# Fetching gathered rows two jobs ahead and running the last batch's transform beside the first expert jobs

## Chip, cores and metric

The kernel runs on one core of a Trainium2 chip. The metric is the device time of one execution in microseconds (us); lower is better.

## What is computed

For `x` of shape (8, 1856, 256) the reference takes the real part of a two-dimensional Fourier transform of each batch, and sends every one of the 14,848 result rows through a two-level mixture of experts:

```python
X = np.fft.fft(np.fft.fft(x, axis=1), axis=2).real     # 8 x 1856 x 256 -> 14848 rows of 256
g = argmax(X @ w_group); e = argmax(X @ w_expert[g])   # 4 groups x 4 experts
h = np.maximum(X @ w1[g, e], 0.0)                      # 256 -> 1024
out[row] = softmax_g * softmax_e * (h @ w2[g, e])      # 1024 -> 256
```

## The kernel before

**Phase 1** (`phase1`) goes through eight batches of 1856 rows. Per batch: `fold` uses the transform's symmetries on VectorE, `s_stage` multiplies by cosine and sine tables (`pu`), `d_stage` does the second transform and the router's logits (`pr`, `pl`), `rows` copies the results into row tiles on ScalarE, and `route` picks expert and place of each row with a chain of small VectorE operations and one group of matmuls (`misc<-oh`), and writes every row to its expert's part of a DRAM table `XS` with indirect DMAs from GpSimd (`scatter`, 14 or 15 tiles of 128 rows a batch). The order of the pieces is written out by hand in strings (`START`, `ORDER0`, `ORDER`, `ORDER7`, `ORDER8`); one letter is one step of one generator. `d_stage` and `route` of batch b run during the `s_stage` of batch b+1; those of the last batch run in a ninth turn with nothing beside them but the first expert's preparation.

**Phase 2** (`phase2`) is a list of *jobs*, each of up to four slots; a slot is 128 rows of one expert. Experts 0 and 1 have early jobs on rows of the first batches (`waves`); every expert has seven fixed slots, from expert 2 on as a job of four and a job of three; twelve overflow slots have weights of their own and come one before each of the experts 2 to 13. A job needs its rows gathered from `XS` into tiles `xg` (a pool of `XGB` buffers), split into two fp16 halves `xh` (a cast on ScalarE, a subtraction on VectorE), and transposed by DMA into `xT` (`turn_steps`); then `layer1` (48 matmuls, `ph`, whose ReLU result `hT` ScalarE and VectorE split) and `layer2` (24 matmuls a slot, `py`, then `y` on ScalarE and an indirect DMA `out<-y`). In the loop of `phase2`, job n runs `layer1(n)` and then `layer2(n-1)`, and meanwhile `prep(n+1)`. `slot_weights` reads each row's weight and number out of `xg` at the start of its job, so an `xg` buffer is held until then. Weights (2 MB an expert, `wst<-w`) are loaded by SyncE, squared and summed on ScalarE (`junk`), and split into fp16 halves (`whl`: a cast on ScalarE, a residual on VectorE).

The helper `InOrder` keeps the order of phase 1 as written; most of phase 2 is ordered by the framework's scheduler ahead of time. On the chip each engine's queue, POOL's and SP's too, is worked through in that order.

```python
g = prep(n + 1)
xT, xgs, ges = xs.pop(n)
cw, toks = self.slot_weights(qp, xgs, ges, inv)   # last reader of job n's xg tiles
next(g, None)                                     # issues the gathers of job n + 1
hT = finish(self.layer1(hp, w, xT, len(slots)), lambda: tick(g, T1 * len(slots)))
```

Of the kernel before, what the change touches and what calls it, by code (L numbers as in the profile page):

```python
# [19 lines left out]
NE, F = 16, 1024  # L20
# [13 lines left out]
XGB = 10  # L34
# [14 lines left out]
START = 'GHGGGZdGHHHGU'  # L49
ORDER0 = 'SSiFSYUYiisFFFFGYSIsilsFFIsFYUdlZRFSSIiRZF'  # L50
ORDER = 'ssRdZFdZsDIDSLStSFlIZZFFDlNDlLZdRlRLRdsNRRSURIRXSdIdRFDiNRLSdDsUdXZSsldtIsNsR'
ORDER7 = 'ISSiZsdDdLZFZDLLZNDZDDDdlDdNWRLIRSWRRsRUDRSRSdIdRSsXSRRiiWlXIRUsRsWRSRsiSRWRXWR'
ORDER8 = 'XIDDiLWXDRWlRLIDDDXDdWRLRRdRdRLtdRURDRRRRRXDDRRRRRRRSRdZXXWXWRW'
# [202 lines left out]
class K:  # L256
# [314 lines left out]
    def nyquist_rows(self, b, U, up):  # L571
# [5 lines left out]
        for i in range(2):  # L577
            self.A.activation(un[:, i], self.UN[:, i], AF.Copy, scale=rat[0:B, 0:1])
            if i:
                if b % 2 == 0:  # L580
                    self.Um[b // 2] = up.tile([P, 2, 2, P], F16, name="Um")
# [83 lines left out]
    def route(self, b, pl):  # L665
# [19 lines left out]
        dd = sm.tile([P, nt, 2, 4], F32, name="dd")  # L685
        mx = sm.tile([P, nt], F32, name="mx")
        m4 = sm.tile([P, nt, 4], F32, name="m4")
# [17 lines left out]
        pe = sm.tile([P, nt, 4, 4], F32, name="pe")  # L705
# [3 lines left out]
        es = sm.tile([P, nt, 4], F32, name="es")  # L709
# [16 lines left out]
        oh = sm.tile([P, 4, 4, nt], F16, name="oh")  # L726
# [19 lines left out]
        op = sm.tile([P, NE, nt], F32, name="offp")  # L746
# [41 lines left out]
    def phase1(self):  # L788
        tc, nc, cp, ps = self.tc, self.nc, self.cp, self.ps
        with tc.tile_pool(name="xq", bufs=4) as xp, tc.tile_pool(name="fft", bufs=1) as fp, \  # L790
                tc.tile_pool(name="u", bufs=2) as up, tc.tile_pool(name="row", bufs=1) as rp:
# [28 lines left out]
            n = waves()[-1][2]  # L820
            for e in range(NEARLY):
                nc.sync.dma_start(
                    out=self.XS[e * CAP:e * CAP + n * P].rearrange("(s p) c -> p s c", p=P),
                    in_=bc(xg[:, :].bitcast(I32), 1, n))

            def run(gens, order, rest=True, keep="N"):

                for k in order:
                    if k == "R":
                        for j in "ZLD":  # L830
                            for _ in gens.pop(j, None) or ():
                                pass
                    if k in self.queues:
                        if self.queues[k]:
                            self.queues[k].pop(0)()
                    elif gens.get(k):
                        next(gens[k], None)
# [11 lines left out]
            for b in range(B + 1):  # L849
# [5 lines left out]
                g["N"] = F  # L855
                if b == W0_AT:
# [5 lines left out]
                if b < B:  # L862
                    Us[b] = up.tile([P, 2, 2, NK], F16, name="U")
                    g["S"] = self.s_stage(b, Us[b])
                    g["U"] = self.nyquist_rows(b, Us[b], up)
# [4 lines left out]
                else:  # L870
                    pl = ps.tile([P, NT * 40 + 20], F32, name="pl", tag="lg")
                    self.row_tiles(b - 1, xp)
                    g["D"] = self.d_stage(b - 1, Us[b - 1], pl)
                    g["L"] = self.leftovers(b - 1, Us.pop(b - 1))
                    g["R"] = self.route(b - 1, pl)
# [4 lines left out]
                order = {0: ORDER0, B - 1: ORDER7, B: ORDER8}.get(b, ORDER)  # L880
                run(g, order, keep="NWXR" if Z else "NWX" if b < B else "N")
            run({}, "sIidddd")


# [163 lines left out]
    def turn_steps(self, qp, xgs, V, A, Q, most=4, bufs=(3, 4)):  # L1048

        n = len(xgs)  # L1050
        xT = qp.tile([P, 4, most * P], F16, name="xT", bufs=bufs[0])
        xT = xT[:, :, 0:n * P]
        for j, xg in enumerate(xgs):
# [3 lines left out]
            V.tensor_tensor(out=xh[:, 1], in0=xg[:, 0:D], in1=xh[:, 0], op=ALU.subtract)  # L1057
# [3 lines left out]
        return xT  # L1061

    def turn(self, qp, xgs):
        return finish(self.turn_steps(qp, xgs, self.nc.vector, self.nc.scalar, self.nc.sync))

    def first_turn(self):
# [4 lines left out]
        self.xT0 = yield from self.turn_steps(self.xp0, self.xg0, self.V, self.A, self.Q, w[2] - w[1], (1, w[2] - w[1]))  # L1071
# [41 lines left out]
    def slot_weights(self, qp, xgs, ges, inv):  # L1113

        t = qp.tile([P, 4], F32, name="cws", bufs=4)
        k = qp.tile([P, 4], I32, name="tok", bufs=4)
        for j, (xg, ge) in enumerate(zip(xgs, ges)):
            self.V.tensor_scalar(out=t[:, j:j + 1], in0=xg[:, D + 1:D + 2], scalar1=inv[:, 0:1], scalar2=None,
                                 op0=ALU.mult)
            self.V.scalar_tensor_tensor(out=k[:, j:j + 1], in0=ge, scalar=BIG, in1=xg[:, D:D + 1],  # L1120
                                        op0=ALU.mult, op1=ALU.add)
        return [[a[:, j:j + 1] for j in range(len(xgs))] for a in (t, k)]

    def phase2(self, wp):
        tc, nc = self.tc, self.nc
        wpa = self.wpa
        with tc.tile_pool(name="wo", bufs=1) as op, \
# [163 lines left out]
```

## Time and profile before

| | us |
|---|---|
| median of 3 runs | 950.77 (947.7 to 952.43) |
| the profiled execution, its own time | 956.92 |
| its span | 955.1 |
| PE busy | 837.9 (88%) |
| ACT, DVE, POOL busy | 597.8, 540.3, 409.7 |

PE is TensorE, ACT ScalarE, DVE VectorE, POOL GpSimd, SP SyncE (which only issues DMAs here). Busy time is a sum over the span; which wait holds PE up in which stretch is read from the waits and the timeline. The granted clock is a share of TensorE's full 2.4 GHz; 0.50 is its lower level, 1.2 GHz.

### The profile page before, as it was taken

What the parts mean: (1) busy time and instruction counts of PE and PEld (TensorE: products, weight loads), DVE (VectorE), ACT (ScalarE), POOL (GpSimd) and SP (SyncE); (2) the same over time, 40 slices, a digit from 0 to 9 for tenths busy, and PEclk for the clock granted to TensorE, in tenths of its full rate; (3) what the DMA queues carried; (4) which work ended last, traced back from release to release, by engine and by line L of the source; (5) the groups of instructions that cost most, each with busy time, mean ns of one, the idle gap of its engine ahead of it and who ended that gap; (6) DMA issues with size and microseconds to landing.
All of it is one profiled execution on the core that took longest, in us unless ns stands there. A gap on an engine that the chain in (4) does not pass through costs nothing. (4 is left out here: it accounts for less than half of the span.)

```text
span 955.1 us, 18094 instructions
## 1 busy us (share of the span) xinstructions
PE 837.9 (88%) x6567; PEld 592.5 (62%) x6567; DVE 540.3 (57%) x1342; ACT 597.8 (63%) x1238; POOL 409.7 (43%) x374
## 2 busy tenths in 40 slices
PE   3798889939798899998898989998999998999996
PEld 1465556717486485757575757575757575766765
DVE  6398775653535766464646555555555655574530
ACT  3477677843657877665767676666666667674631
POOL 1018788777045253434343434343534352533212
PEclk9799999969799999999999999999999999999999
DMA  9824554476725675747474646565656564534001
GB/s 353 282 101 169 194 195 133 149 185 231 255 65 143 196 225 90 225 81 212 81 217 88 205 93 192 109 188 119 185 122 192 116 216 89 163 76 91 34 17 38
DMA packets 110171, 145.95 MB, mean 153 GB/s; under 512 B 76368, under 2 KB 81773, under 8 KB 108288
## 3 DMA queue, kind: packets, MB, share of 16 engines
q1 hardware_dynamic: 92752, 99.96, 36.3%
q0 software_dynamic: 16896, 44.60, 17.3%
q8 instruction: 52, 0.85, 0.4%
q14 instruction: 39, 0.32, 0.1%
q10 hardware_dynamic: 432, 0.22, 0.1%
HBM read 97.18 MB, written 33.29 MB: 137 GB/s over the span
## 5 line engine op out<-in xcount | busy, mean ns | idle before, releaser
L1083 PE MATMUL ph<-xT,whl 128*128 128x384 f16 (+3 forms) x2304 | 378.9, 310 | 40.9 <-DVE hT L1087 26.6
L1099 PE MATMUL py<-whl,hT 128*128 128x256 f16 x2976 | 377.1, 274 | 8.1 <-ACT hT L1086 4.3
L1099 PEld LDWEIGHTS <-hT 128*128 128x128 f16 x2976 | 287.3, 98 | 76.5 <-issue 11.4
L1083 PEld LDWEIGHTS <-whl 128*128 128x128 f16 x2304 | 198.9, 99 | 167.4 <-issue 45.3
L779 POOL DMA_INDIRECT out<-y,tok x124 | 134.5, 1084 | 335.4 <-ACT y L1104 236.0
L1087 DVE SCALAR_TENSOR_TENSOR hT<-ph,hT 128x128 f16<-128x128 f32 (+3 forms) x384 | 184.2, 498 | 117.8 <-ACT hT L1086 114.2
L1086 ACT ACTIVATE hT<-ph 128x128 f16<-128x128 f32 (+3 forms) x384 | 162.3, 446 | 62.9 <-PE ph L1083 60.4
L1042 POOL DMA_INDIRECT xg<-XS,ii_s x100 | 115.0, 1150 | 101.9 <-DVE tok L234 73.6
L234 DVE SCALAR_TENSOR_TENSOR whl<-wst,e_v,whl 128x1024 f16<-128x1024 f32 x112 | 138.8, 1278 | 16.8 <-ACT whl L234 16.0
L1055 ACT CAST xh<-xg 128x256 f16<-128x256 f32 x121 | 48.4, 402 | 154.4 <-DMA xg<-XS,ii_s 89.7
L1057 DVE TENSOR_TENSOR xh<-xg,xh 128x256 f16<-128x256 f32 x121 | 50.7, 422 | 153.5 <-ACT xh L1055 153.5
L234 ACT ACTIVATE whl<-wst,e_v 128x1024 f16<-128x1024 f32 x112 | 122.3, 1139 | 5.7 <-DVE e_v L234 5.6
L234 ACT ACTIVATE junk<-wst 128x1024 bf16<-128x1024 f32 x112 | 118.6, 1059 | 7.7 <-DMA out<-y,tok 6.6
L1104 ACT ACTIVATE y<-py,cws 128x256 f32<-128x256 f32 x124 | 58.1, 474 | 55.5 <-PE py L1099 31.9
L234 PE MATMUL pu<-CS,ghl 128*128 128x464 f16 (+3 forms) x384 | 86.2, 377 | 3.4 <-ACT ghl L234 3.4
L779 POOL DMA_INDIRECT XS<-whl,posi x42 | 50.8, 1210 | 75.1 <-ACT row L234 62.7
L234 PEld LDWEIGHTS <-ghl 128*128 128x128 f16 (+1 forms) x384 | 45.5, 122 | 35.6 <-issue 6.4
L234 PE MATMUL pr<-c,U 128*128 128x256 f16 x336 | 47.7, 278 | 11.7 <-ACT whl L234 6.8
L779 POOL DMA_INDIRECT XS<-row,posi x45 | 51.2, 1137 | 13.6 <-issue 13.1
L234 PEld LDWEIGHTS <-U 128*128 128x128 f16 x672 | 43.3, 98 | 21.2 <-issue 12.9
L234 DVE TENSOR_TENSOR xq<-xq 128x1028 f32<-128x1028 f32 x32 | 38.9, 1224 | 6.7 <-DMA xq<-xq 6.6
L234 ACT CAST U<-pu 128x464 f16<-128x464 f32 (+3 forms) x64 | 32.0, 539 | 6.3 <-PE pu L234 6.1
(148 smaller groups left out, 449.8 us busy)
## 6 DMA issues: line engine op xcount, KB each, us to landing
wst<-w SPq DMA_DIRECT2D x108, 512.0 KB
xq<-xq SPq DMA_DIRECT2D x14, 1028.0 KB
CS<-cs SPq DMA_DIRECT2D x8, 464.5 KB
xq<-xq SPq DMA_DIRECT2D x4, 514.0 KB
wst<-w SPq DMA_DIRECT2D x8, 256.0 KB
xT<-xh SPq DMA_TRANSPOSE x124
out<-y,tok POOLq DMA_INDIRECT x124, 2.8
xg<-XS,ii_s POOLq DMA_INDIRECT x100, 2.9
```

Source lines behind the costliest of these rows:

```text
L234: return self.tc.keep_in_program_order(f(*args, **kw))
L779: ins = self.nc.gpsimd.indirect_dma_start(out=out, out_offset=bass.IndirectOffsetOnAxis(ap=ap, axis=0), in_=in_, in_offset=None, bounds_ch ...
L1042: self.nc.gpsimd.indirect_dma_start(out=xg[:, :].bitcast(I32), out_offset=None, in_=self.XS[:, :], in_offset=bass.IndirectOffsetOnAxis(ap= ...
L1055: A.copy(xh[:, 0], xg[:, 0:D])
L1057: V.tensor_tensor(out=xh[:, 1], in0=xg[:, 0:D], in1=xh[:, 0], op=ALU.subtract)
L1083: nc.tensor.matmul(ph[:, 0:n * P], lhsT=w[:, wl, o:o + P], rhs=xT[:, xl * 2 + c, :], start=i == 0, stop=i == 5)
L1086: nc.scalar.activation(hT[:, f, 0], ph[:, 0:n * P], AF.Relu)
L1087: nc.vector.scalar_tensor_tensor(out=hT[:, f, 1], in0=ph[:, 0:n * P], scalar=0.0, in1=hT[:, f, 0], op0=ALU.max, op1=ALU.subtract)
L1099: nc.tensor.matmul(py, lhsT=hT[:, f, hl, j * P:(j + 1) * P], rhs=w[:, wl, 2048 + f * D:2048 + (f + 1) * D], start=i == 0, stop=i == 23)
L1104: nc.scalar.activation(y, py, AF.Copy, scale=cw)
```

## The change

1. **Rows.** `turn_steps` now also writes a small tile `wt` (each row's number and weight) right after the split, and `slot_weights` reads that; an `xg` buffer is free once its row tile is split. The gathers are moved out of `prep` into `fetch`, which is called for job n+2 at the start of job n. `XGB` falls from 10 to 8. VectorE's small operations go from two a slot to one a slot and two a job.
2. **Memory.** Pools stand on two stacks. The row tiles of the last batch lie on the right, and the right stack is given to `wo` (overflow weights) and `w2s` (raw weights of odd experts from 3) once they are written out; the tiles of the expert jobs take the left space of the transform's tables. The raw weights of expert 1 use the buffer of expert 0.
3. **The last batch.** The ninth turn is gone. `last_rows` steps through `ORDER8` (a `|` ends a step), one step at each `tick` of the first expert jobs. The early jobs now alternate between experts 0 and 1 from the first.
4. **Order.** New order strings; the two DMAs that fill `XS` come a little later; some small pools have one buffer in place of two.

```diff
-XGB = 10
+XGB = 8
-START = 'GHGGGZdGHHHGU'
+START = 'HGGdHGGHHZGUG'
...
-ORDER8 = 'XIDDiLWXDRWlRLIDDDXDdWRLRRdRdRLtdRURDRRRRRXDDRRRRRRRSRdZXXWXWRW'
+ORDER8 = 'sIi|LDD|dDLi|D|sLd|DDL|D|Dd|R|dRR|d|R||R|R|D||RRRR|D|R|RDRdR||R|R|R|RR||||RRLR'
...
             V.tensor_tensor(out=xh[:, 1], in0=xg[:, 0:D], in1=xh[:, 0], op=ALU.subtract)
+            tw = V.scalar_tensor_tensor(out=wt[:, j], in0=ges[j].broadcast_to([P, 2]), scalar=BIG,
+                                        in1=xg[:, D:D + 2], op0=ALU.mult, op1=ALU.add)
...
-    def slot_weights(self, qp, xgs, ges, inv):
+    def slot_weights(self, qp, wt, inv):
+        n = wt.shape[1]
...
+        self.V.tensor_scalar(out=t[:, 0:n], in0=wt[:, :, 1], scalar1=inv[:, 0:1], scalar2=None, op0=ALU.mult)
+        self.V.tensor_copy(out=k[:, 0:n], in_=wt[:, :, 0])
...
+    def last_rows(self):
+        yield from self.run(self.last, ORDER8)
+        for _ in self.last["R"]:
+            pass
+        self.late.close()
...
-            for e in range(NEARLY):
-                for _, r0, r1 in w[:2]:
-                    jobs.append((e, "e", [(e, r) for r in range(r0, r1)]))
-            for _, r0, r1 in w[2:]:
+            for _, r0, r1 in w:
                 for e in range(NEARLY):
...
+                    return "wo", "wo"
+                return ("w2s" if e % 2 and e > 1 else "w"), ("w2" if e % 2 else "wa")
...
             def tick(g, t):
...
                 next(g, None)
+                tail()
...
+            fetch(0)
             finish(prep(0))
+            fetch(1)
...
                 g = prep(n + 1)
-                xT, xgs, ges = xs.pop(n)
-                cw, toks = self.slot_weights(qp, xgs, ges, inv)
-                next(g, None)
+                xT, wt = xs.pop(n)
+                cw, toks = self.slot_weights(qp, wt, inv)
+                fetch(n + 2)
```

Three places show how the instructions move. A number behind a name tells one tile from the next.

**First place: POOL and ACT between two experts in mid-run.** POOL before: scatters of a three-slot job's outputs (`y_5324`, `y_5354`, `y_5384`) and the gathers (`xg`).

```order
L779 DMA out<-y_5324,tok_4931 14848x256
L779 DMA out<-y_5354,tok_4931 14848x256
L1042 DMA xg_5816<-XS_80,ii_s_3537 128x260
L1042 DMA xg_5820<-XS_80,ii_s_3537 128x260
L1042 DMA xg_5824<-XS_80,ii_s_3537 128x260
L1042 DMA xg_6018<-XS_80,ii_s_3537 128x260
L1042 DMA xg_6022<-XS_80,ii_s_3537 128x260
L779 DMA out<-y_5384,tok_4931 14848x256
L779 DMA out<-y_5542,tok_5190 14848x256
```

ACT before, in the four-slot job that follows: the casts `xh` of those gathers stand between the ReLUs `hT`, one output behind the gathers.

```order
L1086 ACTIVATE hT_5411<-ph_5412 128x512
L234 ACTIVATE junk_5423,wacc_5422<-wst_4369 128x1024
L1055 CAST xh_5861<-xg_5816 128x256
L1086 ACTIVATE hT_5411<-ph_5428 128x512
L234 ACTIVATE junk_5423,wacc_5422<-wst_4369 128x1024
L1055 CAST xh_5883<-xg_5820 128x256
L1086 ACTIVATE hT_5411<-ph_5440 128x512
L1055 CAST xh_5905<-xg_5824 128x256
```

POOL now, at the like place (`y_4764` and `y_4794` are outputs of a three-slot job, `y_5089` to `y_5194` those of the next four-slot job).

```order
L781 DMA out<-y_4764,tok_4330 14848x256
L1059 DMA xg_5573<-XS_80,ii_s_3393 128x260
L1059 DMA xg_5577<-XS_80,ii_s_3393 128x260
L1059 DMA xg_5581<-XS_80,ii_s_3393 128x260
L781 DMA out<-y_4794,tok_4330 14848x256
L1059 DMA xg_5585<-XS_80,ii_s_3393 128x260
L781 DMA out<-y_4942,tok_4599 14848x256
L1059 DMA xg_5842<-XS_80,ii_s_3393 128x260
L1059 DMA xg_5846<-XS_80,ii_s_3393 128x260
L781 DMA out<-y_5089,tok_4800 14848x256
```

ACT now, where the casts of these gathers stand.

```order
L1127 ACTIVATE y_5160<-py_5135,cws_4799 128x256
L1127 ACTIVATE y_5194<-py_5169,cws_4799 128x256
L236 ACTIVATE whl_5165<-wst_4593,e_v0_5129 128x1024 x4
L1073 CAST xh_5866<-xg_5573 128x256
L1073 CAST xh_5889<-xg_5577 128x256
L1073 CAST xh_5912<-xg_5581 128x256
L1127 ACTIVATE y_5354<-py_5329,cws_4949 128x256
L1109 ACTIVATE hT_5234<-ph_5235 128x128
```

The gather `xg_5573` now goes out before `y_4794`, and its cast comes behind `y_5194`, six outputs later.

**Second place: DVE in the last batch's choice of experts**, before: the chain that ends in `oh`, which PE's `misc<-oh` waits for.

```order
L234 TENSOR_REDUCE es<-pe 128x60
L234 TENSOR_REDUCE mx<-es 128x15
L234 TENSOR_TENSOR dd<-es,mx 128x15x4
L234 SCALAR_TENSOR_TENSOR m_2611<-dd,c_78 128x60
L234 TENSOR_REDUCE mx<-m_2611 128x15
L1057 TENSOR_TENSOR xh<-xg,xh 128x256
L234 TENSOR_TENSOR oh_2636<-m_2611,mx 128x60
L234 TENSOR_TENSOR xh<-xg,xh 128x256
L1057 TENSOR_TENSOR xh<-xg,xh 128x256
L234 TENSOR_TENSOR oh<-oh_2626,oh_2636 128x240
L234 SCALAR_TENSOR_TENSOR off<-c_78,misc 128x240
```

The same chain now.

```order
L236 TENSOR_REDUCE mx<-m_2815 128x15
L1110 SCALAR_TENSOR_TENSOR hT<-ph,hT 128x384
L236 TENSOR_TENSOR oh_2870<-m_2815,mx 128x60
L1110 SCALAR_TENSOR_TENSOR hT<-ph,hT 128x384
L236 TENSOR_TENSOR pe<-lg,oh_2870 128x240
L236 TENSOR_REDUCE es<-pe 128x60
L236 TENSOR_REDUCE mx<-es 128x15
L236 TENSOR_TENSOR dd<-es,mx 128x15x4
L236 TENSOR_SCALAR cws<-wt,winv 128x3
L236 CAST tok<-wt 128x3
L1110 SCALAR_TENSOR_TENSOR hT<-ph,hT 128x256
L236 SCALAR_TENSOR_TENSOR m_2815<-dd,c_78 128x60
```

The chain now runs between the residuals `hT` of the first three expert jobs.

**Third place: POOL between the phases**, before: row scatters of batch 5 (`row`) and of batches 6 and 7 (`xq`), then outputs, then gathers.

```order
L779 DMA XS<-row,posi 249856x260 x15
L779 DMA XS<-xq,posi 249856x260 x29
L779 DMA out<-y,tok 14848x256 x9
L1042 DMA xg<-XS,ii_s 128x260 x2
L1042 DMA xg<-XS,ii_o 128x260
```

The same stretch now.

```order
L781 DMA XS<-row,posi 249856x260 x15
L781 DMA XS<-xq,posi 249856x260 x14
L781 DMA out<-y,tok 14848x256 x4
L781 DMA XS<-xq,posi 249856x260 x14
L781 DMA out<-y,tok 14848x256
L781 DMA XS<-xq,posi 249856x260
L781 DMA out<-y,tok 14848x256 x3
L1059 DMA xg<-XS,ii_s 128x260 x2
L1059 DMA xg<-XS,ii_o 128x260
```

Five outputs of expert jobs now stand ahead of the last row scatter, and eight of them ahead of the first gather.

## Rows read from the trace of the kernel before

**Rows 1.** Busy time of each engine by stretch of the span; the columns are start and end, length, then PE, PEld, DVE, ACT, POOL busy (with the number of instructions), granted clock, DMA share, GB/s.
```profile
184.00:312.00 128.00, 99.04 (x904) 76.95 (x903) 65.34 (x218) 68.61 (x171) 65.72 (x65) 0.88 0.60 175
312.00:920.00 608.00, 564.65 (x4315) 396.76 (x4316) 343.15 (x821) 398.77 (x797) 238.91 (x201) 0.99 0.55 141
```

**Rows 2.** What PE waited for from 184 to 312 us: what waited <- what ended the wait, total us, times, longest.
```profile
PE misc L234 <- DVE oh L234: 12.6, 1, 12.6
PE pn L1011 <- ACT junk L234: 8.1, 4, 6.4
PE ph L1083 <- DMA xT<-xh: 2.6, 2, 2.3
```

**Rows 3.** The same from 312 us to the end.
```profile
PE ph L1083 <- DVE hT L1087: 25.3, 13, 3.6
PE ph L1083 <- ACT whl L234: 7.9, 8, 1.6
```

**Rows 4.** Timeline of all engines around 508 us: start, length, engine, line, operation, and in brackets the idle time before it and what ended it.
```profile
502.33 1.00 POOL L1042 DMA_INDIRECT xg<-XS,ii_s  x1 [0.31 <-issue]
...
508.06 0.40 ACT L1055 CAST xh<-xg 128x256 f16<-128x256 f32 x1 [3.53 <-DMA xg<-XS,ii_s]
508.37 0.59 ACT L1086 ACTIVATE hT<-ph 128x512 f16<-128x512 f32 x1
...
508.99 0.69 DVE L1087 SCALAR_TENSOR_TENSOR hT<-ph,hT 128x512 f16<-128x512 f32 x1
509.74 1.71 PE L1083 MATMUL ph<-xT,whl 128*128 128x512 f16 x5 [3.14 <-DVE hT L1087]
```

**Rows 5.** Over the whole span: what ACT and POOL waited for in the handling of rows (total us, times, longest).
```profile
ACT xh L1055 <- DMA xg<-XS,ii_s: 89.7, 38, 4.9
ACT xh L1055 <- DMA xT<-xh: 35.9, 18, 4.0
...
POOL xg L1042 <- DVE tok L234: 73.6, 13, 10.8
```

**Rows 6.** Busy time by stretch again: the first and the last of five expert cycles with a clock of 0.96 or 0.97, and between them one with 1.00.
```profile
461.40:509.60 48.20, 44.47 (x340) 31.36 (x340) 26.84 (x65) 31.74 (x65) 19.74 (x16) 0.96 0.59 149
...
655.40:701.60 46.20, 43.28 (x340) 30.75 (x340) 26.62 (x65) 31.46 (x65) 19.87 (x16) 1.00 0.58 158
...
796.50:844.00 47.50, 45.67 (x345) 31.68 (x345) 28.57 (x69) 34.45 (x74) 19.75 (x16) 0.96 0.43 119
```

**Rows 7.** PE's timeline between the phases: first and last tile matmuls of the last batch, its choice matmul, the first expert matmuls, the check of expert 1's weights, the first matmuls of expert 0's slot 6, those of expert 2.
```profile
184.67 0.82 PE L234 MATMUL pr<-c,U 128*128 128x256 f16 x6
...
191.16 0.30 PE L234 MATMUL pl<-RW,Um 128*128 128x20 f16 x6
204.04 0.56 PE L234 MATMUL misc<-oh,c 128*128 128x240 f16 x2 [12.57 <-DVE oh L234]
...
207.47 6.96 PE L1083 MATMUL ph<-xT,whl 128*128 128x384 f16 x24 [2.34 <-DMA xT<-xh]
...
243.48 0.16 PE L1011 MATMUL pn<-wacc,one_b 128*128 128x2 bf16 x1 [6.40 <-ACT junk L234]
...
284.93 1.18 PE L1083 MATMUL ph<-xT,whl 128*128 128x128 f16 x18 [0.23 <-DMA xT<-xh]
...
313.35 5.35 PE L1083 MATMUL ph<-xT,whl 128*128 128x512 f16 x24 [1.64 <-ACT whl L234]
```

**Rows 8.** PE's timeline near the end, at a granted clock of 1.00.
```profile
920.76 3.90 PE L1083 MATMUL ph<-xT,whl 128*128 128x384 f16 x23
...
929.71 17.19 PE L1099 MATMUL py<-whl,hT 128*128 128x256 f16 x156
```

**Rows 9.** Granted clock over the first 24 expert matmuls (PE and PEld busy, clock, DMA share, GB/s).
```profile
207.40:214.40 7.00, 6.93 (x24) 3.14 (x23) 0.57 0.90 163
```

**Rows 10.** From the page: costliest groups on ACT (count | busy us, mean ns of one | idle before).
```profile
L1086 ACT ACTIVATE hT<-ph 128x128 f16<-128x128 f32 (+3 forms) x384 | 162.3, 446 | 62.9 <-PE ph L1083 60.4
...
L234 ACT ACTIVATE whl<-wst,e_v 128x1024 f16<-128x1024 f32 x112 | 122.3, 1139 | 5.7 <-DVE e_v L234 5.6
```

**Rows 11.** SP's queue, from the timeline: the issues of weight DMAs from 234.91 us on (the first four of the twelve are expert 1's).
```profile
234.91 19.66 SPq L992 DMA_DIRECT2D wst<-w  x12
```

**Rows 12.** ACT's timeline behind them: the first and the fourth square (with its sum) of expert 1's weights.
```profile
238.99 1.06 ACT L234 ACTIVATE junk<-wst 128x1024 bf16<-128x1024 f32 x1 [6.64 <-DMA out<-y,tok]
...
243.53 1.06 ACT L234 ACTIVATE junk<-wst 128x1024 bf16<-128x1024 f32 x1
```

**Rows 13.** Row scatters on POOL: one of the longest, and the last one of the last batch with the output scatter behind it.
```profile
85.73 2.03 POOL L779 DMA_INDIRECT XS<-whl,posi  x1 [0.30 <-issue]
...
232.01 0.98 POOL L779 DMA_INDIRECT XS<-xq,posi  x1 [0.30 <-issue]
233.29 0.98 POOL L779 DMA_INDIRECT out<-y,tok  x1 [0.30 <-issue]
```

**Rows 14.** Busy time around the longer scatters and around those of the last batch.
```profile
80.00:112.00 32.00, 24.43 (x226) 17.47 (x225) 25.61 (x56) 21.59 (x47) 25.60 (x22) 0.98 0.63 229
214.00:234.00 20.00, 19.91 (x169) 16.23 (x168) 9.70 (x36) 8.23 (x21) 15.36 (x16) 1.00 0.67 230
```

**Rows 15.** The start on DVE: first and last of eight small operations that the new `START` puts ahead of the first table matmuls.
```profile
16.96 0.16 DVE L234 TENSOR_SCALAR n_ei<-pn 128x8 int32<-128x8 int32 x1
...
18.00 0.18 DVE L234 TENSOR_TENSOR addv<-addv,ew 128x16 f32<-128x16 f32 x1
```

More of the change, by code (lines that the diff above doesn't have):

```diff
@@ L1 @@
+from contextlib import ExitStack
 import numpy as np
@@ L819, in phase1 @@
                 nc.gpsimd.memset(xg, 1.0)
-            n = waves()[-1][2]
-            for e in range(NEARLY):
-                nc.sync.dma_start(
-                    out=self.XS[e * CAP:e * CAP + n * P].rearrange("(s p) c -> p s c", p=P),
-                    in_=bc(xg[:, :].bitcast(I32), 1, n))
-            def run(gens, order, rest=True, keep="N"):
[L828 to L837, printed above, removed]
+            def run(gens, order, rest=True, keep="N"):
+                for _ in self.run(gens, order):
+                    pass
                 for k, g in gens.items():
@@ L848, in phase1 @@
             F, W, X, Z = self.fold(1, xs.pop(1), fp), None, None, None
-            for b in range(B + 1):
+            for b in range(B):
                 g = {"Z": Z, "F": F}
@@ L855, in phase1 @@
                 g["N"] = F
+                if b == 0:
+                    n = waves()[-1][2]
+                    for e in range(NEARLY):
+                        self.Q.dma_start(out=self.XS[e * CAP:e * CAP + n * P].rearrange("(s p) c -> p s c", p=P),
+                                         in_=bc(xg[:, :].bitcast(I32), 1, n))
                 if b == W0_AT:
@@ L879, in phase1, with rows_of, run @@
                 Z = g["R"] if 0 < b < LASTZ else None
-                order = {0: ORDER0, B - 1: ORDER7, B: ORDER8}.get(b, ORDER)
-                run(g, order, keep="NWXR" if Z else "NWX" if b < B else "N")
-            run({}, "sIidddd")
+                run(g, {0: ORDER0, B - 1: ORDER7}.get(b, ORDER), keep="NR" if Z else "N")
+            self.last = self.rows_of(B - 1, Us.pop(B - 1), xp)
+    def rows_of(self, b, U, xp):
+        pl = self.ps.tile([P, NT * 40 + 20], F32, name="pl", tag="lg")
+        self.row_tiles(b, xp)
+        return {"D": self.d_stage(b, U, pl), "L": self.leftovers(b, U), "R": self.route(b, pl)}
+    def run(self, gens, order):
+        for k in order:
+            if k == "R":
+                for j in "ZLD":
+                    for _ in gens.pop(j, None) or ():
+                        pass
+            if k == "|":
+                yield
+            elif k in self.queues:
+                if self.queues[k]:
+                    self.queues[k].pop(0)()
+            elif gens.get(k):
+                next(gens[k], None)
+    def last_rows(self):
+        yield from self.run(self.last, ORDER8)
+        for _ in self.last["R"]:
+            pass
+        self.late.close()
     def slots(self, idx, lim, n, tag, places=True):
@@ L1070, in first_turn @@
         yield
-        self.xT0 = yield from self.turn_steps(self.xp0, self.xg0, self.V, self.A, self.Q, w[2] - w[1], (1, w[2] - w[1]))
+        ges = [self.early[0, r][1] for r in range(*w[1:])]
+        self.xT0 = yield from self.turn_steps(self.xp0, self.xg0, ges, self.V, self.A, self.Q, w[2] - w[1], (1, w[2] - w[1]))
     def layer1(self, qp, w, xT, n):
@@ L1160, in phase2 @@
             for u in range(len(units)):
-                before[u] = next((v for v in reversed(range(u)) if pools(v) == pools(u)), None)
+                before[u] = next((v for v in reversed(range(u)) if pools(v)[1] == pools(u)[1]), None)
             free = lambda u: -1 if before[u] is None else last[before[u]]
@@ L1164, in phase2, with tail @@
             st, ready, infos, xs = {}, {0: self.w0}, {}, {}
-            state = dict(split=None, done=-1, t=0)
+            state = dict(split=None, done=-1, t=0, tail=self.last_rows())
+            def tail():
+                if state["tail"]:
+                    try:
+                        next(state["tail"])
+                    except StopIteration:
+                        state["tail"] = None
+                        for n in ("wo", "w2s"):
+                            pool[n] = later.enter_context(
+                                tc.tile_pool(name=n, bufs=1, side="right", reuse_waits="tile"))
             def load(u):
@@ L1194, in weights, with fetch @@
                 return True
[L1196 removed]
+            def fetch(n):
                 if n >= len(jobs):
```

106 lines of the change are left out of this document (52 added, 54 removed).

## The prediction, on record before the run

> **What bounds the kernel now.** The page gives PE 837.9 us of 955.1, so I first asked where PE is idle, and read busy time by stretch. From 184 to 312 us PE works 99.0 of 128 us at a granted clock of 0.88; from 312 to 920 us it works 565 of 608 at 0.99 [rows 1]. Second, PE's waits. In the first stretch it waits 12.6 us for the last batch's choice of experts, 8.1 for the check of expert 1's weights, 2.6 for a transposition [rows 2]. In the second, 25.3 us in thirteen waits are for the ReLU residual `hT`, and 7.9 for weights' fp16 halves [rows 3].
>
> Third, the timeline around one of the thirteen, to see what made `hT` late [rows 4]: a gather goes out at 502.33 and lands after 508; ACT, which works in order, stands 3.53 us before the cast of that row tile; the ReLU behind it, DVE's residual, and then PE (3.14 us) follow. So PE waits for a gather, through ACT. Over the span that cast waits 89.7 us in 38 waits, and POOL waits 73.6 us in thirteen for `tok`, the last reader of `xg` buffers, before it can gather at all [rows 5]. One long wait in nearly every expert cycle: that is the pattern. Clock follows: a cycle of about 48.2 us has 0.96, one of 46.2 has 1.00, though the third row, with less idle time, has 0.96 as well [rows 6].
>
> **Part B, rows two jobs ahead.** In the order of the change a gather stands before output `y_4794` and its cast behind `y_5194`, six outputs, about one expert cycle, later. Fetch to landing took some 5.7 us [rows 4]; a cycle is over 46 [rows 6]. `XGB` 8 still holds one cycle (seven rows and an overflow slot), and a buffer is now freed by a split that stands, in ACT's order, ahead of the outputs queued behind the gather on POOL. So ACT should find the rows landed. Of the 25.3 us I take 24: a little stays for casts near the overflow slots. The clock: five cycles at 0.96 or 0.97 lose 5 × 0.04 × 48 = 9.6 us; I take 7, as 796.5 to 844 had 0.96 with only 1.8 us idle [rows 6]. **B = 31.** Its bounds: at most 25.3 + 9.6, some 36 with what else follows the gathers; at least 15, if ACT's waits for transpositions (35.9 us, up to 4.0 [rows 5]) hold `hT` up in place of half of it. What is late next is an overflow unit's weights: the 7.9 us stay [rows 3].
>
> **Part A, between the phases.** From PE's first matmul on the last batch's rows, 184.67, to expert 2's first, 313.35, are 128.7 us [rows 7]. The work in them: 6.8 us of transform (to 191.46), and fifteen slots, less one layer 2. A slot's layer 2 is 24 × 17.19/156 = 2.6 us and its layer 1 as 23 × 128x384 in 3.90, so 48 × 0.163/3 = 2.6 [rows 8]: 5.22 a slot. 6.8 + 15 × 5.22 − 2.6 = 82.5; lost are 46.2 us, in the waits of [rows 2] and in clock (the first 24 expert matmuls took 6.96 us in place of 3.9, at 0.57 [rows 9]).
>
> Now the new order, step by step.
> - Expert 0's weights are split ahead of the first expert matmuls, and these now ahead of the last tile matmuls: four casts of 1.14 us [rows 10] and a residual, **+5 us** on the path.
> - The transform then runs among 36 expert matmuls (5.9 us) and ACT's work for them (eight `hT` of 0.45 [rows 10], squares of 1.06 [rows 12], some 3.6 on the path): 184.67 + 5 + 6.8 + 5.9 + 3.6 = 206, before 191.5.
> - The choice matmul stands behind 84 `py`, 48 `ph` of 128x384 and 35 of 128x256: 9.3 + 7.8 + 3.9 = 21 us by [rows 8], and some 3 for the parts of expert 1's weights: **230**, before 204.0 [rows 7]. But PE works meanwhile, where it waited 12.6.
> - A few DVE operations (3 us, an estimate), then fifteen row scatters and one output on POOL, each 1.28 us from the next (232.01 to 233.29 [rows 13]), 20.5 us: the last at **253**, before 232.0.
> - The overflow weights now lie on those row tiles. SP's first load of them waits for the scatters, and behind it in SP's queue stand the next units' loads and, later, the transpositions of the static jobs. By the spacing of the old load of expert 1: issue 2.9 us behind the last scatter [rows 11], first square 4.1 after the issue, fourth 8.6 [rows 12], then a cast, a subtraction and a transposition, some 3 to 5: expert 0's slot 6 starts at about **270**, before 284.93 [rows 7]. Expert 1's raw weights, which were late so far, now come early, into expert 0's buffer.
> - From there to expert 2 I keep the 28.4 us of before: 298.
>
> **A = 15.** Bounds: if PE does nothing but work to slot 6, that starts at 184.67 + 6.8 + 5 + 12 × 5.22 = 259, a gain of 26, 30 with a little of the next stretch. The other end is long scatters. Scatters took 0.98 us beside expert work, DVE busy 9.70 of 20 us, but up to 2.03 in phase 1, DVE busy 25.61 of 32 [rows 13, 14]. Sixteen at the longer size would be 16 × (2.03 + 0.30) = 37 us, 17 more, and A would come to −2; to −5 if the 3 us ahead of them double. I take 1.28, since the last batch's scatters run beside expert work again. A rule of the Trainium skill speaks for the longer size ("SBUF — State Buffer", section "SBUF: two separate sides"): GpSimd writes the descriptors of its own DMAs, and is locked out of a port pair that it shares with VectorE while that runs a 2-port operation. By it A would be near −2 rather than 15; the two rows on the scatters fit it without proving it, as they differ in tile and traffic too.
>
> **Part C, phase 1, and the rest: 0.** Eight small DVE operations (16.96 to 18.2 [rows 15]) now stand ahead of the first table matmuls, about +1.2; other letters of the strings may give as much back. Bounds ±3. The two `XS` fills come a little later, beside transform work; single buffers serve chains that are in order anyway; the fewer small DVE operations (two a job for two a slot, but one a slot added) fall on an engine busy 57%.
>
> **Sum.** 31 + 15 + 0 = 46: 956.9 − 46 = 910.9 against the profiled execution, which lies 6.1 above the median of the runs; against that median, **905 us**. What a measurement can tell from no change is about 0.5%, 4.75 us.
>
> **The rivals.**
> - *PE hardly waits between the phases* (A 28): 892. For it: its work there is only 82.5 us; against it: the overflow weights hang on the last scatter, whatever PE does.
> - *The last batch's rows come late* (A about −1.5, the long scatters above): 921. For it: DVE now has the residuals of twelve slots beside that chain; against it: 0.98 us in 214 to 234.
> - *Transpositions take the gather's place* (B 15): 921. For it the 35.9 us; against it: those waits are short and lie where rows came late as well.
> - *The fetches are not early in effect*, since a buffer comes free no sooner than before: only A, 936; without A, no change. Against it: in the order, splits stand ahead of the queued outputs.
> - *Slower*: a gather that waits on POOL for a split holds up the outputs queued behind it; `y` has four buffers, which cover 4 × 2.6 = 10.5 us; then PE's layer 2 stands. To end above 951 this must eat the whole gain, 46/12 = 3.8 us in each of twelve cycles, so each wait must pass 14.3 us; the longest of POOL's waits was 10.8 [rows 5]. At 5 us a cycle: 965.
>
> **How the numbers follow.** Forecast 905 (895 to 915): 0.55. PE hardly waits: 0.15. Late rows: 0.12. Transpositions: 0.10. Fetches not early: 0.04, half of it at no change. Slower: 0.04. Faster by over 0.5%: 0.55 + 0.15 + 0.12 + 0.10 + 0.02 = 0.94; within: 0.02; slower: 0.04. The range takes in the first four with some 6 us of the bounds of B and C on the outer ones, and leaves out the last two: 885 to 931.
>
> **What would show it.** ACT's waits for gathers fall from 89.7 to under 10 us, PE's 25.3 for `hT` to under 5, expert cycles come to 44 to 45 us at 1.00. The 12.6 and the 6.4 us waits are gone; the choice matmul comes near 230, the last row scatter near 253, a new wait stands before expert 0's slot 6 (262 to 270), and expert 2 starts near 298. I am wrong on B if cycles stay at 47 to 48 us, on A if expert 2 starts after 310, and on C if the last batch's tile matmuls begin more than 3 us off 189.7.

## The result

The changed kernel takes **900.43 us** (median of four runs, 896.56 to 909.29), the kernel before 949.24. The ratio on record is 0.9499, 95% interval 0.9421 to 0.9577 (the two medians alone give 0.9486). The forecast was 905 with a range of 885 to 931; its direction held, and of its two reasons for part B one. Its sum of 46 us is 3 short of the 48.8 measured, and that it came so near is luck, because two terms missed in opposite directions: part B brought some 43 us, not 31, and part A 5 to 10 by medians (7.2 in the profiled executions), not 15.

### The profile page after: what moved, and what is told of

Its sections match the earlier page's. It is cut to its first block, busy times and chain, and to the rows that moved or that the text cites. A ratio compares the mean times of both kernels' runs of the same rounds, so it can differ in the third digit from the quotient of the medians.

```text
span 898.4 us, 18025 instructions
## 1 busy us (share of the span) xinstructions
PE 819.0 (91%) x6567; PEld 594.8 (66%) x6567; DVE 530.5 (59%) x1314; ACT 601.1 (67%) x1238; POOL 387.4 (43%) x372
## 4 chain that ended last, share of the span: by engine, by line
PE 53%; DMA 11%; issue 8%; ACT 3%; POOL 2%; DVE 1%; SPq 0%; POOLq 0%; ACTq 0%; DVEq 0%
PE ph L1106 28%; PE py L1122 25%; DMA xT<-xh 8%; POOL out L781 2%; DMA wst<-w 2%; ACT junk L236 1%; DMA out<-y,tok 1%; ACT whl L236 1%; ACT hT L1109 1%; DVE hT L1110 1%; ACT y L1127 0%; ACT xh L1073 0%; DVE xh L1075 0%; SPq L1081 0%; DMA XS<-xq,posi 0%
## 5 line engine op out<-in xcount | busy, mean ns | idle before, releaser
L1106 PE MATMUL ph<-xT,whl 128*128 128x384 f16 (+3 forms) x2304 | 374.6, 308 | 14.0 <-DMA xT<-xh 10.9
L1122 PE MATMUL py<-whl,hT 128*128 128x256 f16 x2976 | 373.0, 274 | 12.4 <-ACT hT L1109 6.8
L1109 ACT ACTIVATE hT<-ph 128x128 f16<-128x128 f32 (+3 forms) x384 | 164.7, 448 | 92.8 <-PE ph L1106 90.7
L781 POOL DMA_INDIRECT out<-y,tok x124 | 129.8, 1047 | 218.9 <-ACT y L1127 142.2
L781 POOL DMA_INDIRECT XS<-whl,posi x42 | 48.0, 1143 | 74.6 <-DVE Um L236 62.3
L1073 ACT CAST xh<-xg 128x256 f16<-128x256 f32 x121 | 47.5, 403 | 47.6 <-DMA xT<-xh 40.8
```

The costliest lines, as they stand in the source:

```text
L781: ins = self.nc.gpsimd.indirect_dma_start(out=out, out_offset=bass.IndirectOffsetOnAxis(ap=ap, axis=0), in_=in_, in_offset=None, bounds_ch ...
L1073: A.copy(xh[:, 0], xg[:, 0:D])
L1106: nc.tensor.matmul(ph[:, 0:n * P], lhsT=w[:, wl, o:o + P], rhs=xT[:, xl * 2 + c, :], start=i == 0, stop=i == 5)
L1109: nc.scalar.activation(hT[:, f, 0], ph[:, 0:n * P], AF.Relu)
L1122: nc.tensor.matmul(py, lhsT=hT[:, f, hl, j * P:(j + 1) * P], rhs=w[:, wl, 2048 + f * D:2048 + (f + 1) * D], start=i == 0, stop=i == 23)
```

## The profile after

Its profiled execution took 900.23 us, with a span of 898.4. First the busy time by stretch, as in [rows 1] (start and end, length, PE, PEld, DVE, ACT, POOL busy, granted clock, DMA share, GB/s): between the phases, and from expert 2's first matmul to the last two units.

```profile
182.00:306.20 124.20, 93.95 (x905) 77.65 (x905) 66.07 (x236) 69.39 (x174) 74.62 (x72) 0.90 0.70 189
306.20:865.00 558.80, 552.51 (x4328) 398.98 (x4329) 332.88 (x774) 401.35 (x796) 212.70 (x195) 0.99 0.58 151
```

From 306 us on, PE is idle for 6.3 us where it was idle for 43 [rows 1]. These are all of PE's listed waits there (total us, times, longest), against [rows 3]; the 1.6 us end as the stretch begins:

```profile
PE py L1122 <- ACT y L1127: 4.2, 5, 2.5
PE ph L1106 <- ACT whl L236: 1.6, 1, 1.6
PE ph L1106 <- DVE hT L1110: 1.1, 3, 0.7
PE py L1122 <- ACT hT L1109: 0.8, 1, 0.8
```

The 25.3 us for `hT` are 1.1, and the 7.9 for weight halves are 1.6, a single wait. Over the whole span, ACT's two largest waits in its row casts and POOL's largest ahead of a gather, against [rows 5]:

```profile
ACT xh L1073 <- DMA xT<-xh: 40.8, 34, 5.3
ACT xh L1073 <- DMA xg<-XS: 6.3, 3, 3.9
...
POOL xg L1059 <- DVE hT L1110: 103.4, 54, 13.1
```

No cast waits for a POOL gather any more (`xg<-XS` are the early loads from SP), and the wait for `tok` is gone. POOL itself still stands 103.4 us ahead of gathers; it has the time, as no cast waits for it. The profile names `hT`, which reads no `xg`, so what POOL waited for is open. Three expert cycles, against [rows 6]:

```profile
481.20:527.39 46.19, 43.73 (x342) 31.82 (x340) 26.35 (x62) 32.18 (x64) 18.59 (x18) 0.96 0.68 182
527.39:569.34 41.95, 41.95 (x343) 30.94 (x341) 26.19 (x62) 32.07 (x64) 16.23 (x16) 1.00 0.55 142
569.34:611.24 41.90, 41.90 (x343) 30.95 (x341) 26.04 (x62) 31.86 (x64) 17.60 (x17) 1.00 0.70 174
```

In five of the eleven cycles with an overflow slot PE is busy all the time, 41.90 to 41.95 us: the kernel there is PE's work alone. Three more take 42.3 to 42.5, the first two 45.9 and 44.2. The cycle from 481 us still has a clock of 0.96, with one 2.5 us wait in it.

Between the phases, PE's timeline against [rows 7]: the first expert matmuls, the last batch's first tile matmul and choice, two waits ahead of expert 0's slot 6 and its first matmuls, the check of expert 2's weights and expert 2's first matmuls.

```profile
189.31 3.57 PE L1106 MATMUL ph<-xT,whl 128*128 128x384 f16 x11 [7.22 <-DMA xT<-xh]
...
193.28 0.82 PE L236 MATMUL pr<-c,U 128*128 128x256 f16 x6
...
230.09 0.37 PE L236 MATMUL misc<-oh,c 128*128 128x240 f16 x2
...
266.91 0.61 PE L1122 MATMUL py<-whl,hT 128*128 128x256 f16 x2 [5.16 <-ACT hT L1109]
...
277.13 1.97 PE L1106 MATMUL ph<-xT,whl 128*128 128x128 f16 x24 [3.64 <-DMA xT<-xh]
...
304.37 0.16 PE L1028 MATMUL pn<-wacc,one_b 128*128 128x2 bf16 x1 [7.30 <-ACT junk L236]
306.18 8.27 PE L1106 MATMUL ph<-xT,whl 128*128 128x512 f16 x24 [1.64 <-ACT whl L236]
```

The 12.6 us wait is gone, but 7.22 us now stand ahead of the first expert matmuls, 5.16 and 3.64 ahead of slot 6, and 7.30 ahead of expert 2. What the last one waits for, on ACT's timeline: the third and fourth square of expert 2's weights, and the first of the casts between.

```profile
295.69 1.08 ACT L236 ACTIVATE junk<-wst 128x1024 bf16<-128x1024 f32 x1
...
302.20 0.40 ACT L1073 CAST xh<-xg 128x256 f16<-128x256 f32 x1 [5.34 <-DMA xT<-xh]
...
303.18 1.05 ACT L236 ACTIVATE junk<-wst 128x1024 bf16<-128x1024 f32 x1
```

The fourth square shows no wait for its weights; a cast of later rows stood ahead of it in ACT's order, waiting 5.34 us for a transposition. This is a price of part B: early rows bring early casts. Last, POOL, SP and ACT on the chain from the last batch's rows to the overflow weights, against [rows 11 to 13]:

```profile
236.16 0.97 POOL L781 DMA_INDIRECT XS<-xq,posi  x1 [0.79 <-issue]
...
255.37 0.98 POOL L781 DMA_INDIRECT XS<-xq,posi  x1 [0.31 <-issue]
```

```profile
258.09 5.35 SPq L1009 DMA_DIRECT2D wst<-w  x8
```

```profile
263.52 1.06 ACT L236 ACTIVATE junk<-wst 128x1024 bf16<-128x1024 f32 x1 [6.45 <-DMA wst<-w]
...
269.29 1.06 ACT L236 ACTIVATE junk<-wst 128x1024 bf16<-128x1024 f32 x1 [0.83 <-DMA wst<-w]
```

These are the first and the fourth square of the overflow weights. While ACT stands 6.45 us for the first, the `hT` behind it wait too, and PE has its 5.16 us.

## The experiments

Two columns, read from the profiled execution, locate the time: when expert 2's first matmul starts, and the **static part** from there to the end of the span. The last four runs came from two chips (e9 to e11 from one, e12 from another) where the kernel before itself took 1010 and 1008 us in place of 949, so their times stand beside that alone, and their columns beside one another.

| run | median us (lowest to highest) | ratio to before, 95% | expert 2 starts | static part |
|---|---|---|---|---|
| before | 949.24 (946.01 to 952.43) | | 313.4 | 641.8 |
| changed | 900.43 (896.56 to 909.29) | 0.9499 (0.9421 to 0.9577) | 306.2 | 592.2 |
| e1 rows only | 907.12 (901.99 to 908.13) | 0.9547 (0.9484 to 0.9609) | 314.8 | 590.6 |
| e2 one ahead | 897.65 (896.16 to 901.43) | 0.9465 (0.9404 to 0.9526) | 304.3 | 592.9 |
| e3 hold | 942.13 (938.67 to 948.44) | 0.9941 (0.9909 to 0.9973) | 299.2 | 637.9 |
| e4 drain | 895.64 (892.91 to 903.24) | 0.9431 (0.9372 to 0.9490) | 307.2 | 594.3 |
| e5 release | 904.50 (901.73 to 906.86) | 0.9563 (0.9507 to 0.9620) | 314.4 | 585.5 |
| e6 old pools | 905.19 (899.80 to 908.66) | 0.9554 (0.9485 to 0.9623) | 313.0 | 590.9 |
| e7 xh8 | 898.55 (897.42 to 901.78) | 0.9504 (0.9446 to 0.9561) | 308.0 | 587.6 |
| e8 rows late | 914.18 (906.88 to 922.88) | 0.9688 (0.9603 to 0.9773) | 316.9 | 588.2 |
| e9 hold, 16 buffers | 1003.86 (998.40 to 1008.68) | 0.9989 (0.9943 to 1.0034) | 391.4 | 610.5 |
| e10 split first | 985.36 (979.46 to 990.66) | 0.9805 (0.9740 to 0.9869) | 381.5 | 604.9 |
| e11 drain, split first | 989.23 (978.96 to 996.01) | 0.9820 (0.9738 to 0.9902) | 379.1 | 606.9 |
| e12 = e10 again | 986.54 (982.74 to 994.17) | 0.9829 (0.9762 to 0.9896) | 379.9 | 604.0 |

### e1: the rows part alone

The kernel before with `wt`, `fetch(n + 2)` and eight buffers; pools, order strings and ninth turn as before.

> The kernel before with the rows part alone (small tile of numbers and weights, gathers for job n+2 at the start of job n, 8 buffers); order strings, pools and ninth turn as before. If the time of the fetch is what counts, the expert cycles fall from 46-50 us to 42-43, ACT waits under 10 us for gathers, expert 2 still starts near 313 us, and the time is 905 to 910 (some 42 below before). Rival: the new pools and the finer waits of the pools carry the steady part; then cycles stay at 46 or more and the time at 940 or more.

As the first theory said: 907.12 us, the static part as in the changed kernel, the start of expert 2 as before. The rows part is 42 of the 49 us; the new pools have no share in the static part.

### e2: one job ahead

```diff
-                fetch(n + 2)
+                if n != 8:
+                    fetch(n + 2 if n < 8 else n + 1)
```

> The changed kernel, but from the tenth job on the gathers for job n+1, not n+2, go out at the start of job n; buffers are still released by the split. If the fetch's time counts, ACT's waits for gathers come back to 60 us or more, cycles to 46-48 and the time to 935-945. Rival, the early release of the buffers counts: cycles stay at 42-43, the time at 900-904.

The rival was right, and more plainly than it said: apart from the numbers of tiles, every engine's list of instructions is the same as the changed kernel's. As I read it, the scheduler had put the gathers where their buffers allow, wherever the program calls for them. So from the tenth job on "two jobs ahead" does nothing (the jobs before still fetch two ahead here), and this run is a repeat of the changed kernel: 897.65 beside 900.43 shows how closely a median repeats.

### e3: buffers held until the job starts

```diff
-        self.V.tensor_scalar(out=t[:, 0:n], in0=wt[:, :, 1], ...)
-        self.V.tensor_copy(out=k[:, 0:n], in_=wt[:, :, 0])
+        for j, (xg, ge) in enumerate(zip(xgs, ges)):
+            self.V.tensor_scalar(out=t[:, j:j + 1], in0=xg[:, D + 1:D + 2], ...)
+            self.V.scalar_tensor_tensor(out=k[:, j:j + 1], in0=ge, scalar=BIG, in1=xg[:, D:D + 1], ...)
```

> The changed kernel, but weight and number are read out of the gathered row tiles at the start of their job, as before, so that a buffer is held until then; fetch two ahead with 8 buffers stays. If the fetch's time counts: eight buffers are one whole cycle, the buffer that a gather wants was read a job ago, cycles stay near 42 and the time at 898-905. Rival, the early release counts: POOL waits for the numbers again (50 us or more), ACT for gathers, cycles 45-48, the time 925-945.

My theory fell. With the fetch still called two jobs ahead the static part goes from 592 to 638 us. POOL and ACT, over the span:

```profile
POOL xg L1059 <- DVE tok L236: 94.3, 15, 13.0
```

```profile
ACT xh L1072 <- DMA xg<-XS,ii_s: 85.3, 44, 5.1
...
ACT xh L1072 <- DMA xg<-XS,ii_o: 29.5, 10, 3.9
```

One instance on the timeline: the last `tok` of a three-slot job that has just started, the gather of the next cycle's three-slot job, and a cast of its rows.

```profile
506.90 0.15 DVE L236 SCALAR_TENSOR_TENSOR tok<-ge_s,xg 128x1 int32<-128x1 f32 x1
...
506.94 1.04 POOL L1059 DMA_INDIRECT xg<-XS,ii_s  x1 [5.13 <-DVE tok L236]
...
511.89 0.40 ACT L1072 CAST xh<-xg 128x256 f16<-128x256 f32 x1 [1.68 <-DMA xg<-XS,ii_s]
```

The ring of eight is one cycle, the gather stands on POOL as early as its turn in the ring, a cycle ahead, and it goes out in the moment `tok` lets the old rows go. My expectation had the wrong job: the gather whose buffer was free a job ago is not the one that POOL has next. While it waits, outputs queue behind it; PE's largest wait here is `py` for `y`, 30.0 us in 15 waits. That is the mechanism of the prediction's slower rival, in small. New theory: the buffer's release sets the time of the gather, and nothing else in the rows part counts.

### e4: the ninth turn back

```diff
+            while state["tail"]:
+                tail()
             pend = None
             fetch(0)
```

> The changed kernel with the last batch's transform written out in full ahead of the first expert job (a ninth turn again), all else as changed. By the term A of the prediction this costs 15 us: expert 2's first matmul near 321, the time near 915. By the profile of the changed kernel (7 us came from this stretch) it costs 7: 313 and 907. Rival: the overflow weights hang on the last row scatter alone, which now comes sooner (near 232 in place of 255); then expert 2 starts no later than 306 and the time stays at 900.

The rival came out in the time, 895.64, but not for its reason. The last row scatter ends by 240.64, 15.7 us sooner, yet expert 2 starts at 307.19. SP's queue shows why: two transpositions, the second (at 259.16) of gathered rows, now stand ahead of the load of the overflow weights.

```profile
241.66 18.69 SPq L1081 DMA_TRANSPOSE xT<-xh  x2
261.76 2.18 SPq L1009 DMA_DIRECT2D wst<-w  x4
```

The load goes out 3.7 us later than in the changed kernel, and expert 0's slot 6 starts at 278.05, as there (277.13); PE then waits 5.90 us for expert 2's check. Stepping the last batch's transform beside the expert jobs brought nothing that these runs can measure; what rows written earlier are worth, with the load right behind them, was not tried.

### e5: the release alone

The kernel before, with `wt` written after the split and read at the job's start; `prep` gathers one job ahead, ten buffers.

> The kernel before with one thing changed: number and weight go into the small tile right after the split, so a buffer is released there; gathers stay one job ahead, with 10 buffers. Theory, after the hold run: the release alone is what counts. Then cycles fall to 42-43 us, ACT's waits for gathers under 10 us, the time 905-910, like the rows part as a whole. Rival: release and the fetch two ahead are both needed; then cycles stay at 45 or more and the time at 925 or more.

The theory of e3 held: 904.50 us, a static part of 585.5. PE's waits from 314 us on:

```profile
PE ph L1089 <- DVE hT L1093: 3.8, 4, 2.0
PE ph L1089 <- ACT whl L234: 1.7, 1, 1.7
PE py L1105 <- ACT y L1110: 0.3, 1, 0.3
```

Moving one small read gives the whole of part B. The overflow units' weight waits, whose code this run leaves alone, went too.

### e6: expert 1's raw weights and the job order as before

On top of e4:

```diff
-                return ("w2s" if e % 2 and e > 1 else "w"), ("w2" if e % 2 else "wa")
+                return ("w2s" if e % 2 else "w"), ("w2" if e % 2 else "wa")
...
-            for _, r0, r1 in w:
+            for e in range(NEARLY):
+                for _, r0, r1 in w[:2]:
+                    jobs.append((e, "e", [(e, r) for r in range(r0, r1)]))
+            for _, r0, r1 in w[2:]:
                 for e in range(NEARLY):
```

> The changed kernel with the ninth turn back, expert 1's raw weights in the right-hand pool that opens behind the last row scatter (before: memory of the row tiles, too), and the early jobs in the old order; rows part, overflow weights' place and order strings as changed. Theory: what this stretch gained is expert 1's weights coming early; expert 2 then starts at 313-316 and the time is 903-908. Rival: it was the order strings or something else; then expert 2 stays near 307 and the time at 896-900.

The theory held: 905.19 beside e4's 895.64 (the two ranges overlap). Expert 2 starts 5.8 us later, and PE again stands for expert 1's check:

```profile
242.77 0.16 PE L1028 MATMUL misc<-wacc,one_b 128*128 128x2 bf16 x1 [11.64 <-ACT junk L236]
```

So part A's gain is expert 1's weights coming early together with the jobs that alternate; the two were not taken apart, and the order strings were not tried by themselves.

### e7: eight buffers for split rows

```diff
-            xh = qp.tile([P, 2, D], F16, name="xh", bufs=bufs[1])
+            xh = (self.xhp if getattr(self, "xhp", None) else qp).tile([P, 2, D], F16, name="xh", ...)
...
                         for n in ("wo", "w2s"):
+                        self.xhp = later.enter_context(tc.tile_pool(name="xh8", ...))
```

> The changed kernel, with the split rows of the later jobs in eight buffers in place of four (they lie where the last batch's row tiles lay). Theory: the 7.3 us that PE waits for expert 2's weight check come from one cast in ACT's order ahead of the fourth square, which waits 5.3 us for a split buffer that a transposition still reads. With eight buffers the cast finds one, that wait falls under 2 us, expert 2 starts at 298-301, the time is 891-896; ACT's waits on transpositions fall from 40.8 us to under 15. Rival: the square waits for its weights' DMA anyway; expert 2 stays at 305-307, the time at 897-901.

The first theory fell: PE still waits 6.61 us for that check, and the cast ahead of the fourth square still waits, though it has eight buffers:

```profile
303.85 0.40 ACT L1073 CAST xh<-xg 128x256 f16<-128x256 f32 x1 [4.96 <-DMA xT<-xh]
```

SP issues five transpositions in 11.64 us ahead of it (from 291.71 on). Why it still depends on one of them the trace does not tell. ACT's waits for transpositions fell from 40.8 to 31.4 us only, not under 15.

### e8: the last rows later

```diff
-ORDER8 = 'sIi|LDD|...
+ORDER8 = '||||sIi|LDD|...
```

> The changed kernel with four more empty steps ahead of the last batch's transform, so that its rows are written some 8 to 10 us later. By the chain of the prediction (last row scatter, load of the overflow weights, slot 6 of expert 0, expert 2) every us comes back: expert 2's first matmul at 313-316, the time at 906-910. Rival, after the drained run, where the last scatter came 16 us sooner and expert 2 no sooner: this chain has room; expert 2 stays at 305-308, the time at 897-902.

The chain of the prediction held in this direction: the last scatter starts 10.6 us later and expert 2 10.7 us later, one for one. The four times spread from 906.88 to 922.88 (median 914.18), so they bear out the direction and not the size. In e4 earlier rows brought nothing, as the load of the overflow weights did not follow them.

```profile
265.94 0.97 POOL L781 DMA_INDIRECT XS<-xq,posi  x1 [0.31 <-issue]
```

```profile
316.92 7.58 PE L1106 MATMUL ph<-xT,whl 128*128 128x512 f16 x24 [1.80 <-ACT whl L236]
```

### e9: hold, with sixteen buffers

The kernel of e3; gathers alternate between the old eight buffers and eight more in the memory of the last batch's row tiles.

> The hold run again (a gathered row tile is read once more at the start of its job), but with sixteen gather buffers in place of eight, the second eight in the memory of the last batch's row tiles. Theory: a gather waits for the buffer that it reuses, and only that; with a ring of two cycles that buffer was let go a whole cycle ago, POOL's waits for the numbers (94 us with eight) fall under 10 us, ACT's for gathers under 15, cycles to 42-43, the time from 942 to 897-905. Rival: reading the row tile late costs by itself (the gathers are placed late in the order whatever the ring): cycles stay at 45 or more, the time at 925 or more.

In part. The rows of POOL and ACT (ACT's only row casts' wait over 3 us):

```profile
POOL xg L1060 <- DVE tok L236: 77.8, 23, 13.1
```

```profile
ACT xh L1073 <- DMA xT<-xh: 41.8, 21, 4.7
```

POOL's waits for `tok` are 77.8 us, not under 10: the gathers moved further ahead and still wait for their turn in the ring. But no cast waits for a gather, and the static part is 610.5 us against 604.0 to 606.9 for e10 to e12, on chips as slow; with eight buffers holding cost 46 us. More buffers replace the early release nearly fully. The time as a whole shows no gain over before (0.9989), since the stretch ahead of expert 2 is long; that part is not explained.

### e10, e11 and e12: expert 2's split written out earlier

```diff
                 while u not in ready:
                     assert weights()
+                while n == 8 and jobs[n + 1][0] not in ready:
+                    assert weights()
```

> The changed kernel, with the split of expert 2's weights written out at the start of the job before it, so that ACT's order has its four squares and four casts ahead of the casts of later rows. Theory: PE's 7.3 us wait for that check comes from the one row cast that stood ahead of the fourth square and waited 5.3 us for a transposition; now expert 2 starts at 298-301 and the time is 890-896. Rival: the squares wait for something else, or the row casts that now come later hold up expert 2's own rows: expert 2 stays at 304-308, the time at 896-902.

> The same with the last batch's transform written out ahead of the first expert job (no stepping beside the expert jobs). Theory from the drained run (895.6 against 897 to 900 of the changed kernel): the stepping is worth nothing, so this comes to the time of the run before, within 4 us: 888-896. Rival: once the check of expert 2's weights no longer holds PE up, the stepping shows its worth, and this is 5 us or more slower than the run before.

> The same kernel as in the run e10 (the split of expert 2's weights written out at the start of the job before it), since in that call the kernel before itself took 1010 us where it took 949 elsewhere, and every kernel of it lost 60 to 90 us in the first 400 us of the span. On a chip where the kernel before takes 945 to 955: if the check of expert 2's weights is what the boundary lost, expert 2 starts at 298-301 and the time is 890-896; if not, 304-308 and 896-902.

Inconclusive in the time: e12 ran on another chip than e10, but the kernel before took 1008 us there too, and the changed kernel ran on neither. Locally the theory held. PE's wait for that check is gone, and expert 2's first matmuls wait only 1.85 us, for a transposition (granted clock 1.00 in that cycle, 0.94 in the changed kernel):

```profile
381.49 5.34 PE L1106 MATMUL ph<-xT,whl 128*128 128x512 f16 x24 [1.85 <-DMA xT<-xh]
```

From expert 0's slot 6 to here are 25.6 us (25.1 in e12), against 29.1 in the changed kernel, and these 24 matmuls take 5.34 us, not 8.27. e11 and e10 differ by 3.9 us, inside their spread. Whether this version beats the changed one stays open.

## Why the prediction was right, and where not

**What bounds the kernel** was read rightly: PE waited for a gather through ACT's order. e5 shows it with one edit.

**B's cause was half right.** The prediction gave two reasons, the fetch two jobs ahead and the release by the split. Only the second does anything for the static part (e2, e3, e5). Its rival "the fetches are not early in effect, since a buffer comes free no sooner" named what decides; the split released them sooner, so it did not happen.

**B's size was wrong**, 31 forecast with bounds of 15 to 36; e1 and e5 measure 42.3 and 44.0 in medians, and the profiled executions 641.8 − 592.2 = 49.6 (the one of before, at 956.92, was 7.7 us above its median). The step that failed is "what is late next is an overflow unit's weights: the 7.9 us stay". ACT's waiting casts delayed the weight casts as well, so those went with the rest. So did four smaller rows of PE's waits of before, from 313 us on, that the sum left out:

```profile
PE ph L1083 <- DVE whl L234: 3.1, 11, 0.4
PE py L1099 <- ACT y L1104: 2.3, 7, 0.7
PE pn L1011 <- ACT junk L234: 1.6, 5, 0.4
PE py L1099 <- ACT hT L1086: 1.4, 2, 1.0
```

All listed waits were 41.6 us and are 7.7: 33.9. Most of the rest is PE's own busy time for the same matmuls, 565.6 from 313.4 to 921 us before and 552.5 from 306.2 to 865 now: 13.1 us, where 7 were put down for the clock. A cycle at a granted clock of 1.00 was 43.3 busy [rows 6] and is 41.9, so matmuls between waits are also recorded as longer.

**A was mis-sized**, 15 forecast; medians give 5 to 7 (the 48.8 less B), or 10 by e6 beside e4. Its chain can be read point by point: choice matmul 230 forecast, 230.09 found; last row scatter 253, found 255.37; load of the overflow weights 256, found 258.09; slot 6 270, found 277.13; expert 2 298, found 306.18. The step that failed is the one from the load to slot 6: "fourth 8.6, then a cast, a subtraction and a transposition, some 3 to 5". The fourth square came 11.2 us behind the load's issue, as ACT waited for the weights ahead of three of the four, and from its end at 270.35 to slot 6 are 6.8 us. Why the weights landed later than expert 1's did is not shown.

The next step held in length: 28.4 us forecast from slot 6 to expert 2, 29.05 found. But it now holds the 7.30 us wait, without which it would have been shorter. That wait needs no part A, for e1 has it as well:

```profile
312.87 0.16 PE L1011 MATMUL pn<-wacc,one_b 128*128 128x2 bf16 x1 [6.96 <-ACT junk L234]
```

The release alone (e5) does not have it. In e3, whose casts come later, it is 1.24 us, with 5.21 for the first `whl` behind it, and expert 2 starts at 299.2. Whether the earlier fetch or the eight buffers in place of ten add it to the release was not tried. That the stepping would matter found no support either (e4, and e11 beside e10): the gain is expert 1's weights with the order of the jobs (e6).

One sum does not follow from its row: 3.90 us for 23 matmuls is 0.170 each, not 0.163, so PE's work between the phases is some 84.5 us rather than 82.5. No term of the forecast changes by it.

**The long scatters did not come.** Fourteen scatters from 236.16 to 252.81 stand 1.28 us apart, with DVE busy 8.91 of 21 us:

```profile
236.00:257.00 21.00, 21.00 (x217) 18.99 (x215) 8.91 (x39) 7.59 (x21) 15.96 (x17) 1.00 0.29 102
```

These scatters do not test the rule of the Trainium skill that spoke for 2.03 us ("SBUF — State Buffer", section "SBUF: two separate sides"). Yet the same profile has long indirect DMAs elsewhere, and they show that DVE's busy share, by which the prediction told the two sizes apart, was the wrong sign to go by: what counts is the DVE operation that runs as the DMA starts. Here a gather starts while DVE computes a weight residual `whl`:

```profile
499.27 1.27 DVE L236 SCALAR_TENSOR_TENSOR whl<-wst,e_v,whl 128x1024 f16<-128x1024 f32 x1
499.63 2.16 POOL L1059 DMA_INDIRECT xg<-XS,ii_s  x1 [8.16 <-DVE hT L1110]
```

All 17 indirect DMAs of this profile that start at least 0.09 us into such a residual, with 0.5 us or more of it left, take 1.37 to 2.16 us and end 0.85 to 1.25 us behind it; the 78 that meet no DVE operation take 0.97 to 1.05. Nine scatters of phase 1 do the same behind other long DVE operations with two inputs (1.52 to 2.03 us), and the 2.03 us of [rows 13] started 0.09 us into one. None of these ran beside the fourteen. That fits the rule's lock; whether these are 2-port operations the trace does not say.

**C was 0 within its bounds, though my sign for it said otherwise**: the last tile matmuls begin at 193.28, not 189.7. Phase 1's own end did not move so: PE stands from 182.1 on, 7.22 us, for the first job's transpositions. Part A had 5 us of weight casts there instead.

## What to carry to other kernels

Ask of a prefetch what frees its buffer, before asking where it is called: with a scheduler and a ring, the last reader of the old contents sets the time, and one small read at the start of a job can hold a whole cycle back. When one in-order engine is held up, count every wait behind it as its cost, not only the largest row. And look at what the earlier work now stands in front of: here early casts delayed a weight check by 7 us, and in e4 early transpositions delayed a load.

## What was not expected of the hardware

On the two chips of e9 to e12 the time went ahead of expert 2, with instructions as long as elsewhere (scatters 0.97 us in the median, as in the changed kernel): in e10 PE idled 20.2 and 18.1 us in front of `pr` and `pl` matmuls "on issue" (26 and 23 times, up to 2.3 us), rows that the changed kernel's profile does not have. ACT stood 36.0 us in three waits ahead of `whl` and 30.4 in four ahead of `hT` for "remote", a release that comes from no instruction of the profile; the changed kernel has no such wait. The four kernels started expert 2 at 379 to 391 us. The trace names no cause. The kernel before has no profile from these chips, so its static part there is not known.
